# Two and four column tiles for the last attention product of pairs 4 to 31, with reciprocals spread by DMA

## The chip, the cores and the metric

The kernel runs on one core of a Trainium2 chip. The metric is the device time of one execution in microseconds (us); the median of three timed runs stands for a kernel. Engine names as in the profile: PE is TensorE (PEld its weight loads), DVE VectorE, ACT ScalarE, POOL GpSimd, SP SyncE, whose queue (SPq) issues all transfers of this kernel but two.

## What is computed

Linear attention with 8 batches, 8 heads, 576 tokens and head size 64, then a feed-forward layer over all 4608 tokens, all in float32:

```python
q_p, k_p = phi(q), phi(k)        # 128 features: exp(x @ omega.T - |x|^2/2 - row maximum)
kv  = einsum('bhsm,bhsd->bhmd', k_p, v)
z   = sum(k_p, axis=2)
num = einsum('bhsm,bhmd->bhsd', q_p, kv)
den = einsum('bhsm,bhm->bhs', q_p, z)[..., None] + 1e-06
x   = (num / den)                # heads side by side: 4608 x 512
h   = x @ w_in                   # 512 -> 2048
out = (h * erf(softplus(h))) @ w_out
```

## The kernel before

**Work.** Attention goes by pairs of heads: 32 pairs, numbered n = 4 * batch + p. The feed-forward layer goes by six blocks of tokens (`SUPERS`; the first two have 576 tokens each, the others 864), each in four quarters of the hidden size; it is most of TensorE's work. Its matmuls are float32r in three terms (high x high, high x low, low x high), with tiles h, hX, hY, hZ for the first product and o, oX, oY, oZ for the second. The attention's matmuls are float32.

**One pair.** `load` brings q, k and v; `project` makes the features (tiles ppk, ppq in PSUM; after the exponential fk, fq in SBUF). `key_values` multiplies the features of the keys with v and a column of ones into the PSUM tile kvp: for each head 64 columns of values and one column, z. It does so in two column tiles, the array's left half for features 0 to 63, its right half for 64 to 127. `kvhigh` copies kvp into the SBUF tile kh, with z repeated 64 times for each head, so that kh is 2 x 128 columns. `turn` transposes fq in three steps (pt in PSUM, qh in SBUF, 128 features x 1152 tokens of the two heads).

**The last product, which the change touches**, is in `attend`. There are four products for each pair, one for each head j and half t of its tokens (`SPANS`: 288 each): weights kh[:, j] (128 features x 128 columns), moving qh (288 columns). The result nd, a PSUM bank, holds 64 rows of numerators and 64 equal rows of denominators. `log_den` takes the logarithm of the 64 denominator rows and writes it to the other 64 partitions, those of the numerators, in the SBUF tile rc; `exp_den` takes exp(-x) of both heads' at once; `divide` multiplies the numerators in PSUM by it into xs, on 64 partitions at a time.

```python
def log_den(self, rc, nd, j, w):
    num, den = rows(j)
    act.activation(rc.ap[num], nd.ap[den, :w], AF.Ln, bias=eps[den])
def divide(self, x, nd, rc, j, o, c, w):
    num = rows(j)[0]
    dve.tensor_mul(x.ap[num, o:o + w], nd.ap[num, c:c + w], rc.ap[num, c:c + w])
```

`split` makes high and low parts (xh, xl, xc) of xs for a block of tokens, before the first product of that block.

**What sets the order.** Every step is declared with `pl.op`: the engines that may do it and the time that it is thought to take, what it reads and writes, and for some a due time (`plan`). `Plan.order` runs a list schedule over all steps when the program is built: each engine takes the ready step that is due first, steps without a due time get theirs from their successors, and a step that needs a buffer waits for a free one (`SLOTS`, `CAPS`; kh and qh have one buffer each). Each engine then carries out its steps in the order found, in order. SyncE's queue is ordered in the same way; weight fetches may be issued up to `AHEAD` = 40.09 us before they are due, and the time of a transfer is taken from `BANDWIDTH`. `JITTER` adds a fixed pseudo-random perturbation to the due times in the stretches that it lists.

The due time of an attention step is `pair_time(n, x)`: the start of pair n's period plus x times the period (at most 33 us) times 1.2. The period is 33.4 us for pairs 4 to 7, 20.7 for 8 to 15, 42.1 for 16 to 19, 24.5 for 20 to 27 and 40.9 for 28 to 31; pairs 0 to 3, before the feed-forward layer begins, have 11.4. The four products of pair n are due at x = 0.75, 0.80, 0.85 and 0.90, key_values at 0.28, turn from 0.5 on. PSUM has 8 banks.

Of the kernel before, what the change touches and what calls it, by code (L numbers as in the profile page):

```python
# [71 lines left out]


COST = dict(mm=0.132, proj=0.222, half=0.156, tr=0.109, kv=1.35, table=1.3)
BANDWIDTH = 270e3
LAG = {"T": 0.33914999999999995, "A": 0.258, "V": 0.24975, "G": 0.2994, "S": 0.3024}
SLOTS = dict(w=8, g=11, u=2, f=2, mx=3, sq=3, v=1, qh=1, ql=1, kh=1, kl=1, xs=12, xh=2, xl=2,
             os=4, ps=8)
# [239 lines left out]
def whole_(n):  # L318
# [1 line left out]
    return n < WHOLE or WHOLE2[0] <= n < WHOLE2[1]  # L320


JITTER = ((186.1, 206.1, 4, 581), (227.5, 727.5, 4, 5), (648.5, 748.5, 1, 6), (712.0, 762.0, 2, 7),
# [34 lines left out]
AHEAD = 40.09  # L358

SPANS = ((0, 288), (288, 288))  # L360
# [16 lines left out]
BY = 30.39  # L377
RPOOL = SPOOL = "g"
VOS = 5
TAIL = [("V", 0.69, -1e9)]  # L380
LATE = 52.68
LOADS = 1e9
# [9 lines left out]
def build(emit):  # L392
# [246 lines left out]
    def key_values(n, t0):  # L639
        a = pairs[n]  # L640
        f, v = a["fk"], a["v"]
        kvp = a["kvp"] = pl.tile("ps", "kvp" + a["nm"], [P, 512], F32, "att", early(n))
        pl.op("kv", [("T", COST["kv"], -1e9)], lambda e: E.key_values(kvp, f, v),
              reads=[(f, i) for i in range(NC)] + [(v, 0)], writes=[(kvp, 0)], plan=pair_time(n, t0))
        whole = whole_(n)
        kh = a["kh"] = pl.tile("kh", "kh" + a["nm"], [P, 2, P], F32 if whole else F32R)
        kl = a["kl"] = kh if whole else pl.tile("kl", "kl" + a["nm"], [P, 2, P], F32R)
        pl.op("kvhigh", [("V", 0.6, -1e9), ("A", 0.7, -1e9)], lambda e: E.kv_high(e, kh, kvp),
              reads=[(kvp, 0)], writes=[(kh, 0)])
        if not whole:  # L650
            pl.op("kvrest", [("V", 0.6, -1e9)], lambda e: E.kv_rest(kl, kvp, kh),
                  reads=[(kvp, 0), (kh, 0)], writes=[(kl, 0)])

    def turn(n, t0):
# [5 lines left out]
        for i in range(3):  # L660
# [5 lines left out]
            if not whole:  # L666
                pl.op("turnrest", [("V", 0.56, -1e9)], lambda e, i=i, pt=pt: E.turn_rest(ql, qh, pt, i),
                      reads=[(pt, 0), (qh, i)], writes=[(ql, i)])

    def attend(n, t0):  # L670
        a = pairs[n]
        for t, (c0, w) in enumerate(SPANS):
            rc = pl.tile(f"rc{t}", f"rc{a['nm']}_{t}", [P, w])
            nds = [pl.tile("ps", f"nd{a['nm']}_{j}_{t}", [P, 512], F32, "att", early(n)) for j in range(2)]
            for j, nd in enumerate(nds):
                c = range((j * S + c0) // 384, (j * S + c0 + w - 1) // 384 + 1)
                pl.op("nd", [("T", w / 600 if whole_(n) else 3 * max(0.111, 0.012 + w / 2400), -1e9)],
                      lambda e, j=j, c0=c0, w=w, nd=nd:
                      E.attend(nd, a["kh"], a["kl"], a["qh"], a["ql"], j, c0, w),
                      reads=[(a["kh"], 0), (a["kl"], 0)] + [(a["qh"], i) for i in c]  # L680
                      + [(a["ql"], i) for i in c], writes=[(nd, 0)],
                      plan=pair_time(n, t0 + 0.1 * t + 0.05 * j))
            for j, nd in enumerate(nds):
                pl.op("ndlog", [("A", 0.25 + 0.00083 * w, -1e9)],
                      lambda e, j=j, w=w, nd=nd, rc=rc: E.log_den(rc, nd, j, w),
                      reads=[(nd, 0)], writes=[(rc, j)], set="exp")
            pl.op("ndexp", [("A", 0.2 + 0.00083 * w, -1e9)], lambda e, rc=rc: E.exp_den(rc),
                  reads=[(rc, 0), (rc, 1)], writes=[(rc, 0), (rc, 1)], set="exp")
            for i, h, o, at0, n0 in pieces(a["b"], c0, w):
                k = (i, a["p"], h)  # L690
                if k not in xs:
                    xs[k] = pl.tile("xs", "xs%d_%d_%d" % k, [P, SUPERS[i][0]]), []
                x, keys = xs[k]
                for j, nd in enumerate(nds):
                    key = (n, t, at0, j)
                    keys.append(key)
                    pl.op("divide", [("V", 0.15 + 0.00105 * n0, -1e9)],
                          lambda e, j=j, x=x, o=o, at0=at0, n0=n0, nd=nd, rc=rc:
                          E.divide(x, nd, rc, j, o, at0, n0),
                          reads=[(nd, 0), (rc, j)], writes=[(x, key)],  # L700
                          plan=pair_time(n, t0 + 0.1 * t) + DIVIDE)
# [35 lines left out]
    def attention(n):  # L737
        if n == 0:
            load(0, "k")
            project(0, "k", 0.0)  # L740
            load(0, "q")
        project(n, "q", 0.15)
        if n + 1 < N:
            load(n + 1, "k")
        key_values(n, 0.28)
        if n + 1 < N:
            project(n + 1, "k", 0.0)
            load(n + 1, "q")
        turn(n, 0.5)
        attend(n, 0.75)  # L750


    gran = {}
# [276 lines left out]
def tile_attention_moe(ctx: ExitStack, tc: tile.TileContext, qT, kT, qR, kR, qN, kN, vP, omT, w1, w2, out):  # L1030
# [68 lines left out]
    class Emit:  # L1099
# [140 lines left out]
        def kv_rest(self, kl, kvp, kh):  # L1240
            for (dst, src), (hi, _) in zip(self.kv_parts(kvp, kl), self.kv_parts(kvp, kh)):
                dve.tensor_sub(dst, src, hi.bitcast(F32))

        def turn(self, pt, f, i):
            for c in range(3):
                pe.transpose(out=pt.ap[:, c * P:(c + 1) * P], in_=f.ap[:, 3 * i + c, :], identity=ident)
# [162 lines left out]
```

## Time and profile before

| | before |
|---|---|
| runs, us | 1014.33, 1015.59, 1019.1 |
| median, us | 1015.59 |
| span of the profiled execution, us | 1013.4 |
| PE, DVE, ACT, POOL busy | 98%, 78%, 69%, 63% |
| bytes moved by DMA | 235.87 MB |
| mean granted TensorE clock | 0.998 |

The profile shows one execution. Its span runs from its first instruction to its last; its time as the runs count it isn't given beside it, so the span is set against the median. Busy time of an engine is the time covered by its instructions; for PE the ends of matmuls are modelled and overlap, so steps from start to start say more than durations. A float32 matmul appears as two records, a float32r matmul and a transpose as one.

### The profile page before, as it was taken

The numbers are of one execution on the slowest core, as the hardware profiler recorded it, in microseconds if no ns is written. First come the engines' busy times: TensorE is split into PE (matmuls) and PEld (weight loads), VectorE is DVE, ScalarE is ACT, GpSimd is POOL, SyncE is SP. The second block draws the span as 40 slices with busy tenths as digits, with TensorE's granted clock in tenths as the row PEclk, the third lists the DMA queues.
The fourth block names the chain that finished last, engine by engine and source line by source line (L and its number), as shares of the span: only waits on it lengthen the run. The fifth ranks groups of instructions, "written<-read, shape, count | busy, mean of one in ns | idle before, by whom it ended". The sixth has DMA issues, their size and how long they took to land.

```text
span 1013.4 us, 19460 instructions
## 1 busy us (share of the span) xinstructions
PE 995.4 (98%) x7108; PEld 926.1 (91%) x7108; DVE 788.7 (78%) x1278; ACT 695.3 (69%) x1307; POOL 636.1 (63%) x477
## 2 busy tenths in 40 slices
PE   8999999999999999999999999999999999999998
PEld 7899889989999899999999899999999999999997
DVE  5799878996677878676897778789787788687654
ACT  7979787686785975766768685868548665746560
POOL 3535433866668857475894848489575687677530
PEclk9999999999999999999999999999999999999999
DMA  8376778588687597576766867676677556686761
GB/s 214 102 254 245 254 237 325 192 306 302 227 279 240 166 320 289 186 279 230 256 215 216 310 228 226 217 226 204 225 274 242 186 177 219 227 293 213 232 205 70
DMA packets 102366, 235.87 MB, mean 233 GB/s; under 512 B 11520, under 2 KB 12032, under 8 KB 102272
## 3 DMA queue, kind: packets, MB, share of 16 engines
q1 hardware_dynamic: 102112, 234.57, 69.2%
q8 instruction: 57, 0.93, 0.4%
q14 instruction: 37, 0.30, 0.1%
q10 hardware_dynamic: 160, 0.07, 0.0%
HBM read 191.59 MB, written 42.99 MB: 231 GB/s over the span
## 4 chain that ended last, share of the span: by engine, by line
PE 88%; DVE 6%; DMA 4%; ACT 1%; SPq 1%; issue 1%; DVEq 0%; ACTq 0%
PE hX L1047 15%; PE o L1047 14%; PE oX L1047 12%; PE h L1047 8%; PE hY L1047 7%; PE oY L1047 6%; PE nd L1047 5%; PE ppq L1047 4%; PE hZ L1047 4%; PE ppk L1047 3%; PE kvp L1047 3%; PE oZ L1047 3%; PE pt L1047 2%; DMA st<-w 2%; DVE st L1047 1%; DMA uk<-kT 1%
## 5 line engine op out<-in xcount | busy, mean ns | idle before, releaser
L1047 PE MATMUL o<-gh,w 128*128 128x288 f32 (+1 forms) x704 | 176.0, 324 | 3.3 <-DVE w L1047 1.8
L1047 PE MATMUL hX<-xh,wb 128*128 128x432 f32 x512 | 171.4, 368 | 0.0
L1047 POOL TENSOR_TENSOR hs<-gs,hs 128x864 f32<-128x864 f32 (+1 forms) x44 | 95.5, 2190 | 94.5 <-ACT gs L1047 83.0
L1047 PEld LDWEIGHTS o<-gh,w 128*128 128x128 f32 x704 | 122.4, 189 | 8.2 <-DVE w L1047 2.5
L1047 PE MATMUL h<-xh,w 128*128 128x288 f32 x512 | 123.4, 312 | 2.2 <-ACT w L1047 1.0
L1047 PE MATMUL o<-gl,w 128*128 128x288 f32 (+1 forms) x352 | 110.3, 313 | 0.0
L1047 PE MATMUL oX<-th,wb 128*128 128x432 f32 x312 | 101.4, 364 | 0.0
L1047 PEld LDWEIGHTS hX<-xh,wb 128*128 128x128 f32 x512 | 96.2, 188 | 5.2 <-DVE hs L1047 0.2
L1047 PE MATMUL hX<-xl,wb 128*128 128x432 f32 x256 | 91.8, 359 | 0.7 <-DVE xl L1047 0.7
L1047 PEld LDWEIGHTS h<-xh,w 128*128 128x128 f32 x512 | 86.8, 189 | 5.9 <-ACT w L1047 1.2
L1047 POOL TENSOR_TENSOR uq<-uq 128x288 f32<-128x288 f32 (+1 forms) x50 | 45.7, 934 | 72.8 <-DMA uq<-qN 31.8
L1047 ACT ACT_TABLE_LOAD x68 | 87.2, 1283 | 1.9 <-PEq L1400 0.7
L1047 PE MATMUL hY<-xh,wb 128*128 128x432 f32 x256 | 88.2, 372 | 0.0
L1047 ACT ACTIVATE fk<-ppk,mxk 128x128 f32<-128x128 f32 x288 | 81.9, 378 | 5.7 <-DVE mxk L1047 5.2
L1047 ACT ACTIVATE fq<-ppq,mxq 128x128 f32<-128x128 f32 x288 | 78.2, 384 | 8.0 <-DVE mxq L1047 7.5
L1047 ACT ACTIVATE rc<-nd,eps 64x288 f32<-64x288 f32 x128 | 63.5, 496 | 27.7 <-PE nd L1047 25.1
L1047 PE MATMUL nd<-qh,kh 128*128 128x288 f32 x256 | 78.0, 409 | 3.8 <-DVE qh L1047 2.9
L1047 DVE TENSOR_TENSOR xs<-nd,rc 64x288 f32<-64x288 f32 (+1 forms) x160 | 61.6, 393 | 24.6 <-ACT rc L1047 17.8
L1047 ACT ACTIVATE hs<-hX 128x432 f32<-128x432 f32 x64 | 33.8, 531 | 67.4 <-PE hX L1047 63.3
L1047 POOL TENSOR_TENSOR tl<-gs,th 128x864 fp32r<-128x864 f32 x32 | 71.1, 2241 | 9.7 <-ACT th L1047 3.5
L1047 PE MATMUL h<-xl,w 128*128 128x288 f32 x256 | 75.7, 296 | 0.0
L1047 ACT ACTIVATE gs<-hs 128x1728 f32<-128x1728 f32 (+1 forms) x48 | 69.0, 1479 | 0.3
(144 smaller groups left out, 2770.3 us busy)
## 6 DMA issues: line engine op xcount, KB each, us to landing
wb<-wdc SPq DMA_DIRECT2D x232, 256.0 KB, 3.8
wb<-wdw SPq DMA_DIRECT2D x174, 256.0 KB, 3.9
w<-wdw SPq DMA_DIRECT2D x44, 512.0 KB, 6.2
st<-w SPq DMA_DIRECT2D x32, 512.0 KB, 6.0
wdw<-w SPq DMA_DIRECT2D x32, 512.0 KB, 5.0
wdc<-c SPq DMA_DIRECT2D x32, 512.0 KB, 4.6
v<-vP SPq DMA_DIRECT2D x32, 325.0 KB, 4.6
uk<-kR SPq DMA_DIRECT2D x24, 320.0 KB, 4.7
```

What stands on the lines that cost most here:

```text
L1047: return tc.keep_in_program_order(method(*args, **kwargs))
```

## The change

- For pairs 4 to 31 (`n >= APART`) the last product is taken apart. kh is now 128 numerator columns (64 for each head) and 64 columns that hold z of each head 32 times.
- `denominators`: four matmuls of 32 columns, one for each head and half of the tokens, in four column tiles, into one PSUM bank dn. One logarithm and one exponential follow over all 128 partitions x 288. The result is stored in DRAM (147,456 bytes) and read back by two transfers, one for each head, each of which puts the two rows of that head on 64 partitions (tile rb).
- `numerators`: for each half of the tokens two matmuls of 64 columns, one for each head, in two column tiles, into one bank; then one multiplication (or more, where a block of tokens ends within) on all 128 partitions. They are due at x = 1.15 and 1.25 and are declared after the key_values of the next pair. Their banks count apart from the others' (at most two).
- `BANDWIDTH` goes from 270e3 to 310e3, and the list in `JITTER` is another: 31 entries in place of 115. So the order of all steps changes.

```diff
-BANDWIDTH = 270e3
+BANDWIDTH = 310e3
...
+APART = 4
+NDCAP = 2
+NUM0 = 1.15
...
+        if n >= APART:
+            kh = a["kh"] = pl.tile("kh", "kh" + a["nm"], [P, 3 * D])
+            pl.op("kvhigh", [("V", 0.49, -1e9), ("A", 0.45, -1e9)], lambda e: E.kv_apart(e, kh, kvp),
+                  reads=[(kvp, 0)], writes=[(kh, 0)])
+            return
...
+    def denominators(n, t0):
...
+        pl.op("nd", [("T", 0.49, -1e9)], lambda e: E.denominators(dn, a["kh"], a["qh"], w),
+              reads=everything, writes=[(dn, 0)], plan=pair_time(n, t0))
+        rc = pl.tile("rc0", "rc" + a["nm"], [P, w])
+        pl.op("ndlog", [("A", 0.5, -1e9)], lambda e: E.log_dens(rc, dn, w), reads=[(dn, 0)],
+              writes=[(rc, 0)], set="exp")
+        pl.op("ndexp", [("A", 0.44, -1e9)], lambda e: E.exp_den(rc), reads=[(rc, 0)], writes=[(rc, 0)],
+              set="exp")
+        rd = pl.tile("wdr" + a["nm"], "wdr" + a["nm"], [P, w])
+        pl.op("rstore", [("S", 0.1, 1e9)], lambda e: E.fetch(rd.ap, rc.ap), reads=[(rc, 0)],
+              writes=[(rd, 0)], size=P * w * 4)
+        rb = pl.tile("rb", "rb" + a["nm"], [P, 2, w])
+        for j in range(2):
+            pl.op("rfetch", [("S", 0.1, 1e9)], lambda e, j=j: E.spread(rb, rd, j), reads=[(rd, 0)],
+                  writes=[(rb, j)], size=P * w * 4)
+        a["rb"] = rb
+
+    def numerators(n, t0):
...
+        for t, (c0, _) in enumerate(SPANS):
+            nd = pl.tile("ps", f"nd{t}{a['nm']}", [P, 512], F32, "nd" if NDCAP else "att", NDCAP or early(n))
+            pl.op("nd", [("T", 0.49, -1e9)],
+                  lambda e, c0=c0, nd=nd: E.numerators(nd, a["kh"], a["qh"], c0, w),
+                  reads=everything, writes=[(nd, 0)], plan=pair_time(n, t0 + 0.1 * t))
...
     def attend(n, t0):
+        if n >= APART:
+            denominators(n, t0)
+            return
...
         key_values(n, 0.28)
+        if n > APART:
+            numerators(n - 1, NUM0)
...
         attend(n, 0.75)
+        if n + 1 == N:
+            numerators(n, NUM0)
...
+        def denominators(self, dn, kh, qh, w):
+            r = D // 2
+            for g in range(4):
+                c = P + g // 2 * r
+                pe.matmul(dn.ap[g * r:(g + 1) * r, :w], lhsT=kh.ap[:, c:c + r],
+                          rhs=qh.ap[:, g * w:(g + 1) * w], start=True, stop=True)
+
+        def numerators(self, nd, kh, qh, c0, w):
+            for j in range(2):
+                c = slice(j * S + c0, j * S + c0 + w)
+                pe.matmul(nd.ap[j * D:(j + 1) * D, :w], lhsT=kh.ap[:, j * D:(j + 1) * D],
+                          rhs=qh.ap[:, c], start=True, stop=True)
+
+        def log_dens(self, rc, dn, w):
+            act.activation(rc.ap, dn.ap[:, :w], AF.Ln, bias=eps)
+
+        def spread(self, rb, rd, j):
+            rows = rd.ap.rearrange("(j t r) c -> j r t c", j=2, t=2)[j, 0:1]
+            sp.dma_start(rb.ap[j * D:(j + 1) * D], rows.broadcast_to([D, 2, rows.shape[-1]]))
+
+        def divide_both(self, x, nd, rb, t, o, c, w):
+            dve.tensor_mul(x.ap[:, o:o + w], nd.ap[:, c:c + w], rb.ap[:, t, c:c + w])
```

## Rows read from the trace of the kernel before

**Rows 1.** The page's first part: span, then busy time of each engine.

```profile
span 1013.4 us, 19460 instructions
PE 995.4 (98%) x7108; PEld 926.1 (91%) x7108; DVE 788.7 (78%) x1278; ACT 695.3 (69%) x1307; POOL 636.1 (63%) x477
```

**Rows 2.** Busy time by stretches: length, each engine, granted clock, DMA share, GB/s.

```profile
50.00:200.00 150.00, 144.79 (x1238) 137.73 (x1239) 130.12 (x223) 116.83 (x246) 74.20 (x68) 0.99 0.72 250
200.00:355.00 155.00, 152.40 (x1351) 141.97 (x1350) 121.46 (x227) 114.59 (x254) 110.62 (x103) 1.00 0.74 253
355.00:835.00 480.00, 480.00 (x3244) 440.86 (x3241) 382.34 (x615) 333.55 (x606) 330.56 (x226) 1.00 0.71 237
```

**Rows 3.** TensorE in order of time around three last products: start, duration, instructions.

```profile
516.88 0.36 PE L1047 MATMUL hY<-xl,wb 128*128 128x432 f32 x1
517.08 0.35 PE L1047 MATMUL hY<-xh,wb 128*128 128x432 f32 x1
517.27 0.65 PE L1047 MATMUL nd<-qh,kh 128*128 128x288 f32 x2
517.54 0.57 PE L1047 MATMUL hY<-xh,wb 128*128 128x432 f32 x1
517.95 0.36 PE L1047 MATMUL hY<-xl,wb 128*128 128x432 f32 x1
...
522.17 0.36 PE L1047 MATMUL hY<-xh,wb 128*128 128x432 f32 x1
522.37 1.14 PE L1047 MATMUL nd<-qh,kh 128*128 128x288 f32 x4
523.12 0.57 PE L1047 MATMUL hY<-xh,wb 128*128 128x432 f32 x1
523.54 0.36 PE L1047 MATMUL hY<-xl,wb 128*128 128x432 f32 x1
```

**Rows 4.** The same view around one kvp; its last two records apart.

```profile
503.08 0.35 PE L1047 MATMUL oY<-bh,wb 128*128 128x432 f32 x1
503.36 1.38 PE L1047 MATMUL kvp<-v,fk 128*64 128x130 f32 x36
504.51 0.23 PE L1047 MATMUL kvp<-v,fk 128*64 128x65 f32 x2
504.67 0.46 PE L1047 MATMUL oZ<-bh,wb 128*128 128x432 f32 x1
504.97 0.35 PE L1047 MATMUL oZ<-bl,wb 128*128 128x432 f32 x1
```

**Rows 5.** The same view: first and last run of nd, pairs 4 to 31.

```profile
60.30 0.65 PE L1047 MATMUL nd<-qh,kh 128*128 128x288 f32 x2
...
831.08 0.65 PE L1047 MATMUL nd<-qh,kh 128*128 128x288 f32 x2
```

**Rows 6.** Groups of ScalarE: form, count, busy us, mean ns, idle before.

```profile
L1047 ACT ACTIVATE rc<-nd,eps 64x288 f32<-64x288 f32 x128 | 63.5, 496 | 27.7 <-PE nd L1047 25.1
L1047 ACT ACTIVATE rc<-rc 128x288 f32<-128x288 f32 x64 | 28.4, 444 | 2.0
```

**Rows 7.** Groups of VectorE, the multiplications.

```profile
L1047 DVE TENSOR_TENSOR xs<-nd,rc 64x288 f32<-64x288 f32 x96 | 43.4, 453 | 19.7 <-ACT rc L1047 15.8 <-PE nd L1047 1.9
L1047 DVE TENSOR_TENSOR xs<-nd,rc 64x144 f32<-64x144 f32 x64 | 18.3, 302 | 4.9 <-ACT rc L1047 2.0 <-PE nd L1047 1.9
```

**Rows 8.** DMA: packets, the main queue, two kinds of issue (median us to landing).

```profile
DMA packets 102366, 235.87 MB, mean 233 GB/s; under 512 B 11520, under 2 KB 12032, under 8 KB 102272
q1 hardware_dynamic: 102112, 234.57, 69.2%
wdw<-w SPq DMA_DIRECT2D x32, 512.0 KB, 5.0
uq<-qT SPq DMA_DIRECT2D x3, 96.0 KB, 2.8
```

**Rows 9.** TensorE's waits from 50 to 355 us, first and last of eleven.

```profile
PE o L1047 <- DVE w L1047: 1.8, 3, 1.0
...
PE hZ L1047 <- ACT fq L1047: 0.2, 1, 0.2
```

**Rows 10.** In order of time, VectorE and TensorE near 352 us.

```profile
349.64 2.98 DVE L1047 TENSOR_TENSOR xl<-xc,xh 128x1728 fp32r<-128x1728 f32 x1
...
351.66 0.35 PE L1047 MATMUL hX<-xh,wb 128*128 128x432 f32 x1
352.68 0.46 PE L1047 MATMUL hX<-xl,wb 128*128 128x432 f32 x1 [0.67 <-DVE xl L1047]
```

**Rows 11.** VectorE's waits: us in total, times, longest.

```profile
DVE xs L1047 <- ACT rc L1047: 17.8, 19, 2.2
```

More of the change, by code (lines that the diff above doesn't have):

```diff
@@ L320, in whole_ @@
     return n < WHOLE or WHOLE2[0] <= n < WHOLE2[1]
-JITTER = ((186.1, 206.1, 4, 581), (227.5, 727.5, 4, 5), (648.5, 748.5, 1, 6), (712.0, 762.0, 2, 7),
[34 rows of a table removed]
+JITTER = ((126.7, 226.7, 8, 485), (605.4, 615.4, 4, 265), (421.4, 471.4, 8, 168),
[10 rows of a table added]
 AHEAD = 40.09
@@ L668, in turn, with place, bank @@
                       reads=[(pt, 0), (qh, i)], writes=[(ql, i)])
+    def place(n, t, c0, w, nds, part):
+        a = pairs[n]
+        for i, h, o, at0, n0 in pieces(a["b"], c0, w):
+            k = (i, a["p"], h)
+            if k not in xs:
+                xs[k] = pl.tile("xs", "xs%d_%d_%d" % k, [P, SUPERS[i][0]]), []
+            part(k, i, o, at0, n0)
+    def denominators(n, t0):
+        a = pairs[n]
+        w = SPANS[0][1]
+        everything = [(a["kh"], 0)] + [(a["qh"], i) for i in range(3)]
+        def bank(name):
+            return pl.tile("ps", name + a["nm"], [P, 512], F32, "att", early(n))
+        dn = bank("dn")
+        pl.op("nd", [("T", 0.49, -1e9)], lambda e: E.denominators(dn, a["kh"], a["qh"], w),
[13 more added lines that the diff above has]
+        a["rb"] = rb
@@ new lines, in numerators, with part @@
+    def numerators(n, t0):
+        a = pairs[n]
+        w, rb = SPANS[0][1], a["rb"]
+        everything = [(a["kh"], 0)] + [(a["qh"], i) for i in range(3)]
+        for t, (c0, _) in enumerate(SPANS):
[3 more added lines that the diff above has]
+                  reads=everything, writes=[(nd, 0)], plan=pair_time(n, t0 + 0.1 * t))
+            def part(k, i, o, at0, n0, t=t, nd=nd):
+                x, keys = xs[k]
+                keys.append((n, t, at0))
+                pl.op("divide", [("V", 0.15 + 0.00105 * n0, -1e9)],
+                      lambda e: E.divide_both(x, nd, rb, t, o, at0, n0),
+                      reads=[(nd, 0), (rb, 0), (rb, 1)], writes=[(x, keys[-1])],
+                      plan=pair_time(n, t0 + 0.1 * t) + DIVIDE)
+            place(n, t, c0, w, nd, part)
@@ L1242, in kv_rest, with kv_apart @@
                 dve.tensor_sub(dst, src, hi.bitcast(F32))
+        def kv_apart(self, e, kh, kvp):
+            s = kvp.ap[:, :2 * P].rearrange("p (j d) -> p j d", j=2)[:, :, :D1]
+            copy(e, kh.ap[:, :P].rearrange("p (j d) -> p j d", j=2), s[:, :, :D])
+            copy(e, kh.ap[:, P:].rearrange("p (j d) -> p j d", j=2),
+                 s[:, :, D:].broadcast_to([P, 2, D // 2]))
+        def denominators(self, dn, kh, qh, w):
[16 more added lines that the diff above has]
+            dve.tensor_mul(x.ap[:, o:o + w], nd.ap[:, c:c + w], rb.ap[:, t, c:c + w])
         def turn(self, pt, f, i):
```

44 rows, old and new, of the table JITTER are left out of this document.

## The prediction

> **What bounds the kernel now.** I read the page's first part, then busy time by stretches, then the order of time around two places. The page and the stretches [rows 1, 2]: TensorE is busy 995.4 of 1013.4 us, and from 355 to 835 us it is busy 480.00 of 480.00 at the full granted clock. In the two stretches before, from 50 to 355 us, it stands still for 5.2 + 2.6 = 7.8 us in all. VectorE and ScalarE have a quarter of their time free. So whatever adds a microsecond to TensorE's own sequence adds one to the end, and whatever frees another engine can give back 7.8 us at most outside the first 50 us, which pairs 0 to 3 fill and the change leaves alone.
>
> Next, the price of one last product [rows 3]. The float32r matmuls around it step by 0.20 us. From hY at 517.08 to the second hY after it at 517.95 lie 0.87 us, which hold two such steps and one product: 0.47. From 522.17 to 523.54 lie 1.37 us with two products: 0.97, so 0.485 each. That is 288 float32 columns at 1.68 ns, and nothing is lost on the way in or out. The records last 0.40 us each and overlap; only starts are used.
>
> Then the one place where the kernel already uses two column tiles, kvp [rows 4]. From oY at 503.08 to the second oZ at 504.97 lie 1.89 us; without two steps, 1.49. Each half of the array takes one product of 130 columns and eight of 65, 650 columns, 1.09 us at 1.68 ns; the halves in turn would need 2.19. So they run together, and 0.40 us is lost around them. Part of the loss is seen at the ends. kvp starts 0.28 after oY, 0.08 more than a step. Its last records start at 504.51 and need some 0.055 for half a product of 65 columns, but oZ starts at 504.67: 0.105. The next oZ comes after 0.30, 0.10 more than a step. Together 0.285. The rest, 0.115, is first-weight time or a small loss in each of nine steps. A full-width product between full-width neighbours pays none of this. I take 0.34 us for one visit to a tiled arrangement of long products, between 0.285 and 0.40.
>
> The Trainium skill ("TensorEngine Tiling (Array Packing)", Tiling Modes) says that changing the tiling mode, not just the tile, drains TensorE, and in its Overview that columns of at most 32 allow up to four times the speed. By that speed alone the sum below would be 13.6 us less time; the trace agrees with the drain as well, at 0.285 to 0.40 us a visit, which turns the sign.
>
> **TensorE's columns.** A pair now has four products, 1.94 us [rows 3]. Afterwards it has three steps of 288 columns: the four denominators side by side, and twice two numerators side by side. If tiles run fully together that is 1.455 us. Over 28 pairs: 54.3 before, 40.7 after, -13.6 us. Two halves at full speed are shown by kvp, though both halves read the same columns there; four, each with other columns, are not shown. If they ran two and two, the denominators cost 0.97 and 13.6 us come on top; one after the other, 40.7 on top. Nothing excludes either, but the nearest row runs together, so I take 0.485.
>
> **TensorE's visits.** The three steps of a pair are due at 0.75, 1.15 and 1.25 of its period, so they stand apart unless the order happens to join them: 84 visits at most. How often neighbours join can be counted now: the 112 products of pairs 4 to 31 stand in 86 runs, the first at 60.30 and the last at 831.08 [rows 5], so 26 of 84 neighbours, 31%, are joined, with dues 0.05 of a period apart. The two numerator steps are due 0.1 apart; I take 13%, 4 joins. By the file's due times, in the 20 pairs whose period is under 34 us, numerators(n-1) is due about 1 us after key_values(n), which is in the same two-column arrangement; 31% of those is 6 joins. That leaves 74 visits x 0.34 = 25.2 us. Bounds: 28 visits x 0.285 = 8 and 84 x 0.40 = 34. Net TensorE: 25.2 - 13.6 = +11.6 us, between -6 and +20.
>
> **ScalarE and VectorE.** Now a pair has four logarithms of 496 ns and two exponentials of 444 [rows 6]; afterwards one of each at full height, for which I take the same times: 1.93 us less, 54 us over 28 pairs. Multiplications take 43.4 + 18.3 us, 1.93 us a pair [rows 7]; at full height there are half as many, 27 us less in all. The copy of kvp loses half of its second part. None of this is on the path from 355 us on. Of the 7.8 us before that I give back 3.
>
> **DMA.** Each of the 28 pairs stores 147 KB and reads it back twice: 84 transfers, 12.4 MB, 5.3% of the 235.87 MB that the page counts; the queue's share of 69.2% [rows 8] becomes some 73%. SyncE's queue is in order, so the store waits there for the exponential and the two reads for the store, with weight fetches queued behind. Those are issued up to 40 us ahead, and from 50 to 355 us TensorE's eleven kinds of wait, 8.0 us in all, end with VectorE or ScalarE and none with a transfer [rows 9]. I cost this at nothing; the cover is that lead, and without it TensorE would pay the store's landing, 2.8 to 5.0 us [rows 8], for each pair.
>
> **Added waits and moved steps.** The numerators leave pair n for a place after key_values(n+1). TensorE does not wait there for the reciprocals, since its matmuls read kh and qh alone; the multiplication on VectorE does. From the denominators on that is 0.50 + 0.44 on ScalarE and two landings, from 2.8 (96 KB) to 5.0 us (512 KB): 6.5 to 10.9 us, against a distance in due time of 0.4 of a period x 1.2: 9.9 us in pairs 8 to 15, 11.8 in 20 to 27, 15.8 in the others. It fits, with little to spare; behind a late multiplication stand all of VectorE's drains of PSUM. kh and qh have one buffer, so kvhigh(n+1) and the first turn copy now wait for numerators(n); TensorE passes those in order, and kh is needed 0.47 of a period later. xs is complete 10 to 16 us later. That bites at the change of token blocks: at 351.66 hX already waits 0.67 us for an xl that VectorE ends at 352.6 [rows 10]. For five such changes I add 2 us in all, from 0 to 8.
>
> **Order.** The bandwidth constant and the perturbations change the whole order. What it can take away are the 7.8 us above; what it adds could be as much. I take nothing, 8 us either way.
>
> **Sum.** -13.6 + 25.2 - 3 + 2 = +10.6 us. The profiled span of 1013.4 becomes 1024.0; the median of the runs, 1015.6, is 2.2 above that span, so 1026 us.
>
> **Rivals.**
> (a) The order joins the steps. With 40 visits in all, 1.4 a pair, the change breaks even on TensorE. The least is 28: the four-column step needs a visit of its own, and both numerator steps are entered from kvp; 28 x 0.34 = 9.5, a gain of 4. With the 3 us given back these are 1012.6 and 1008.5, and the order's 8 us around them. Below 34 visits it is faster by 0.5%. For it: 31% of neighbours join today. Against: the dues of the two numerator steps are twice as far apart as those of today's neighbours.
> (b) The gain on the other engines about cancels the visits: all 7.8 us come back and a visit costs 0.285 (74 x 0.285 = 21 us): 21 - 13.6 - 7.8 = 0, 1015. Against: nothing outside 50 to 355 us can come back.
> (c) The reciprocals come late. If queueing on ScalarE and SyncE adds 3 us in the 16 pairs with 9.9 to 11.8 us, VectorE stands still for up to 48 us, and with half of it passed on through PSUM TensorE loses 24: 1050; with a quarter, 1038. For it: the multiplications already wait 17.8 us for ScalarE's reciprocals now [rows 11]. Against: that is 0.9 us at a time, and the dues leave 9.9 us.
> (d) Four streams of different columns don't run together: 13.6 us more, 1040. Against it kvp, for two.
>
> **How the numbers follow.** My forecast 0.46 (1019 to 1034), (a) 0.17, (b) 0.14, (c) 0.15, (d) 0.08. The time is 1026. The range takes the forecast, (b), (d), nearly all of (a) and the lower part of (c): 1007 to 1042. A difference under 0.5% (5 us) can't be told from no change here. Faster by more than that: two thirds of (a), 0.11, and with the order's 8 us some of (b), 0.06: 0.17. Within 0.5%: the rest of (a), 0.06, of (b), 0.08, and the forecast's low end, 0.05: 0.19. Slower: 0.64.
>
> **What would show it.** In the profile after: nd's and the denominators' starts 0.485 us apart for full 288 columns with neighbours 0.3 us late around them, some 74 separate tiled visits besides kvp's; TensorE still near 98% busy; ScalarE some 54 and VectorE some 27 us less; no TensorE wait for DMA. I am wrong if the steps stand side by side (fewer than 40 visits), if a visit costs under 0.2 us with 288 columns, or if TensorE shows new waits on VectorE's drains.

## The result and the profile after

| | before | after |
|---|---|---|
| runs, us | 1014.33 to 1019.1 (4) | 1022.99, 1026.25, 1026.36, 1027.67 |
| median, us | 1016.37 | 1026.3 |
| ratio, 95% interval | | 1.0095 [1.0067, 1.0123] |
| profiled span, us | 1013.4 | 1021.2 |

The change costs 10 us, 1.0%. A fourth run of the kernel before, 1017.14, is counted in here. The profiled execution of after is the one of 1022.99, the lowest of the four; the spans of the others are 1024.5 to 1025.9. Of all runs below one, 1046.53 us of e10 at a mean granted clock of 0.907, is in the slower state and left out of its median.

The page's first part of after, beside [rows 1]:

```profile
span 1021.2 us, 19871 instructions
PE 1002.1 (98%) x7332; PEld 899.5 (88%) x7332; DVE 776.3 (76%) x1226; ACT 649.4 (64%) x1200; POOL 637.5 (62%) x457
```

ScalarE and VectorE have 46 and 12 us less to do; TensorE is at 98% as before, over a longer span. Busy time by stretches, beside [rows 2]:

```profile
50.00:200.00 150.00, 144.38 (x1270) 132.20 (x1269) 123.25 (x220) 111.25 (x230) 71.94 (x63) 0.99 0.80 268
200.00:355.00 155.00, 153.87 (x1404) 137.36 (x1402) 113.15 (x206) 104.30 (x232) 105.52 (x94) 0.99 0.79 271
355.00:835.00 480.00, 479.42 (x3348) 419.96 (x3347) 373.46 (x575) 304.34 (x536) 326.41 (x220) 1.00 0.76 248
```

From 355 to 835 us TensorE is as full as before (479.42 of 480), with ScalarE 29 and VectorE 9 us lighter: freed time on engines that weren't the bound. TensorE in order of time around one step of numerators and one of denominators, beside [rows 3]:

```profile
575.46 0.36 PE L1092 MATMUL hY<-xl,wb 128*128 128x432 f32 x1
575.66 0.35 PE L1092 MATMUL hY<-xh,wb 128*128 128x432 f32 x1
575.94 0.71 PE L1092 MATMUL nd<-qh,kh 128*64 128x288 f32 x4
576.58 0.46 PE L1092 MATMUL hZ<-xh,wb 128*128 128x432 f32 x1
576.88 0.35 PE L1092 MATMUL hZ<-xl,wb 128*128 128x432 f32 x1
...
641.82 0.36 PE L1092 MATMUL oX<-th,wb 128*128 128x432 f32 x1
642.11 0.69 PE L1092 MATMUL dn<-qh,kh 128*32 128x288 f32 x8
642.73 0.46 PE L1092 MATMUL oX<-th,wb 128*128 128x432 f32 x1
643.03 0.35 PE L1092 MATMUL oX<-tl,wb 128*128 128x432 f32 x1
```

Numerators: from 575.66 to 576.88 lie 1.22 us; two float32r steps of 0.20 and one step of 288 float32 columns, 0.485, are 0.88, so 0.34 is lost. Denominators: 641.82 to 643.03 are 1.21, again 0.33 lost, although eight records, four products of different columns, lie in that one step. So four column tiles do run together, and each visit pays on the way in (the start comes 0.08 to 0.09 later than a step) and on the way out.

**A ledger of TensorE.** I took every step from start to start, subtracted the time of its columns, and counted what is over around a run of tiled products as the visit's loss (the median of its kind), all else as the rest: waits, and columns at half clock (the last section shows such a stretch; each of 3.4 us costs some 1.7). The rest is what is left over, so the ledger always adds up.

| profiled execution | columns | visits: loss (count) | rest | first to last matmul |
|---|---|---|---|---|
| before | 947.2 | 34.6 (80) | 23.6 | 1005.4 |
| after | 933.8 | 55.3 (127) | 24.0 | 1013.0 |

The 7.6 us between the two are -13.4 of columns, +20.7 of visits and +0.4 of the rest (rounded).

### The profile page after: what moved, and what is told of

Its sections match the earlier page's. It is cut to its first block, busy times and chain, and to the rows that moved or that the text cites. A ratio compares the mean times of both kernels' runs of the same rounds, so it can differ in the third digit from the quotient of the medians.

```text
span 1021.2 us, 19871 instructions
## 1 busy us (share of the span) xinstructions
PE 1002.1 (98%) x7332; PEld 899.5 (88%) x7332; DVE 776.3 (76%) x1226; ACT 649.4 (64%) x1200; POOL 637.5 (62%) x457
## 3 DMA queue, kind: packets, MB, share of 16 engines
q1 hardware_dynamic: 114208, 246.96, 73.5%
## 4 chain that ended last, share of the span: by engine, by line
PE 89%; DVE 7%; DMA 2%; issue 1%; ACT 1%; SPq 0%; DVEq 0%
PE o L1092 15%; PE hX L1092 14%; PE oX L1092 12%; PE h L1092 10%; PE hY L1092 7%; PE oY L1092 6%; PE ppq L1092 5%; PE ppk L1092 4%; PE nd L1092 4%; PE kvp L1092 4%; PE hZ L1092 3%; PE oZ L1092 3%; PE pt L1092 2%; PE dn L1092 2%; DVE gs L1092 1%; DVE hs L1092 1%
## 5 line engine op out<-in xcount | busy, mean ns | idle before, releaser
L1092 PE MATMUL o<-gh,w 128*128 128x288 f32 (+1 forms) x704 | 169.1, 319 | 2.2 <-ACT w L1092 1.2
L1092 PE MATMUL hX<-xh,wb 128*128 128x432 f32 x512 | 166.5, 366 | 0.7 <-DVE hs L1092 0.7
L1092 POOL TENSOR_TENSOR hs<-gs,hs 128x864 f32<-128x864 f32 (+1 forms) x50 | 102.9, 2080 | 101.7 <-ACT gs L1092 78.8
L1092 PE MATMUL h<-xh,w 128*128 128x288 f32 x512 | 119.0, 308 | 3.4 <-DVE w L1092 1.9
L1092 POOL TENSOR_TENSOR uq<-uq 128x288 f32<-128x288 f32 (+1 forms) x46 | 41.6, 924 | 80.0 <-DMA uq<-qN 40.0
L1092 POOL TENSOR_TENSOR tl<-gs,th 128x864 fp32r<-128x864 f32 x34 | 80.1, 2378 | 18.3 <-ACT th L1092 9.0
L1092 PE MATMUL hY<-xh,wb 128*128 128x432 f32 x256 | 83.8, 365 | 0.0
L1092 ACT ACTIVATE gs<-gs 128x1728 f32<-128x1728 f32 (+1 forms) x48 | 69.0, 1481 | 0.3
L1092 PEld LDWEIGHTS o<-gl,w 128*128 128x128 f32 x352 | 66.8, 190 | 0.8
L1092 DVE TENSOR_TENSOR os<-oX,os 128x432 f32<-128x432 f32 x86 | 51.0, 602 | 20.2 <-PE oX L1092 20.1
```

Source lines behind the costliest of these rows:

```text
L1092: return tc.keep_in_program_order(method(*args, **kwargs))
```

## The experiments

The times are medians; the ratios are to the kernel before on the same chip (1016.58 for e1, e3, e4 and e5, 1014.96 for e2, e6 and e7, 1015.93 for e8 to e10). The ledger of all of them:

| run | median | ratio [95%] | profiled span | visits (count) | rest |
|---|---|---|---|---|---|
| e1 before, new order | 1037.38 | 1.0197 [1.0144, 1.025] | 1035.5 | 35.7 (78) | 44.6 |
| e2 after, old order | 1054.47 | 1.0376 [1.0346, 1.0406] | 1055.7 | 56.4 (127) | 56.9 |
| e3 before, split columns | 1041.9 | 1.0254 [1.0238, 1.027] | 1038.9 | 67.5 (165) | 16.3 |
| e4 after, full width | 1011.11 | 0.9947 [0.9928, 0.9965] | 1006.9 | 34.7 (80) | 29.5 |
| e5 after, no transfers | 1022.03 | 1.0063 [1.0044, 1.0082] | 1019.6 | 55.3 (127) | 22.5 |
| e6 numerators beside kvp | 1020.81 | 1.0051 [1.0028, 1.0075] | 1018.5 | 43.7 (104) | 32.8 |
| e7 also denominators beside ppq | 1026.5 | 1.0115 [1.0075, 1.0154] | 1023.0 | 39.1 (81) | 41.8 |
| e8 as e6, order made for it | 1017.77 | 1.0023 [1.0005, 1.004] | 1011.1 | 43.0 (100) | 26.0 |
| e9 as e8, another order | 1022.72 | 1.0074 [1.0053, 1.0096] | 1021.2 | 42.0 (95) | 37.1 |
| e10 as e7, order made for it | 1025.92 | 1.0088 [1.0059, 1.0118] | 1024.6 | 38.8 (79) | 43.8 |

Columns are 947.2 us in e1 and e3, 933.8 in all others.

**e3: what does a visit cost, with nothing else changed?** Before's kernel in before's order; each last product becomes two half-width ones side by side over the same columns.

```diff
-                pe.matmul(nd.ap[:, :w], lhsT=kh.ap[:, j, :], rhs=qh.ap[:, c], start=True, stop=True)
+                for h in (slice(0, D), slice(D, P)):
+                    pe.matmul(nd.ap[h, :w], lhsT=kh.ap[:, j, h], rhs=qh.ap[:, c], start=True, stop=True)
```

> The kernel before with each of its last products issued as two products of 64 weight columns side by side, over the same 288 columns, in the same order: the column time stays, and 90 visits to the two-column arrangement come in. Theory: a visit costs 0.345 us as in the trace after, four of them in the first 50 us: 28 to 31 us more, 1044 to 1047 us. Rival (a visit is hidden, or its cost belongs to kvp's short products): within 5 us of the kernel before.

25.3 us slower. TensorE around one product of e3:

```profile
530.33 0.35 PE L1047 MATMUL hY<-xh,wb 128*128 128x432 f32 x1
530.61 0.71 PE L1047 MATMUL nd<-qh,kh 128*64 128x288 f32 x4
531.25 0.46 PE L1047 MATMUL hY<-xh,wb 128*128 128x432 f32 x1
531.55 0.36 PE L1047 MATMUL hY<-xl,wb 128*128 128x432 f32 x1
```

530.33 to 531.55 is 1.22 us where [rows 3] have 0.87. The median over the 62 single products that stand alone is 0.354 lost. In all, visits cost 33 us more, so the price is real. 7 us of the rest went away: 1.7 of them is the one stretch at half clock that before has and e3 has not, 1.2 are waits (12.9 us in place of 14.1), and about 2 are waits of the first 50 us that the ledger counts as visits here. The time is 2 us below the theory's 1044 to 1047 and far from the rival's.

**e4: after without the visits.** The same steps in the same order, same columns, full width.

```diff
...
-            r = D // 2
-            for g in range(4):
-                c = P + g // 2 * r
-                pe.matmul(dn.ap[g * r:(g + 1) * r, :w], lhsT=kh.ap[:, c:c + r],
-                          rhs=qh.ap[:, g * w:(g + 1) * w], start=True, stop=True)
+            pe.matmul(dn.ap[:, :w], lhsT=kh.ap[:, P:2 * P], rhs=qh.ap[:, :w], start=True, stop=True)
...
-            for j in range(2):
-                c = slice(j * S + c0, j * S + c0 + w)
-                pe.matmul(nd.ap[j * D:(j + 1) * D, :w], lhsT=kh.ap[:, j * D:(j + 1) * D],
-                          rhs=qh.ap[:, c], start=True, stop=True)
+            pe.matmul(nd.ap[:, :w], lhsT=kh.ap[:, :P], rhs=qh.ap[:, c0:c0 + w], start=True, stop=True)
```

> The kernel after in the same order, but each of its three steps is one full-width product over 288 columns: same column time, no visits, and the transfers and the work of the other engines stay. It leaves out the numerators of each pair's second head and three of the four denominators. Theory: the 20.8 us that the visits of these steps cost in the trace after go, 1003 to 1008 us, faster than the kernel before by about 1%. Rival (the order, the transfers or late reciprocals make it slower): 1022 us or more.

15.2 us faster than after, and 5.4 faster than before. TensorE around one numerator product of e4:

```profile
541.70 0.35 PE L1092 MATMUL oX<-th,wb 128*128 128x432 f32 x1
541.89 0.65 PE L1092 MATMUL nd<-qh,kh 128*128 128x288 f32 x2
542.16 0.58 PE L1092 MATMUL oZ<-bh,wb 128*128 128x432 f32 x1
542.58 0.36 PE L1092 MATMUL oZ<-bl,wb 128*128 128x432 f32 x1
```

541.70 to 542.58 is 0.88 us, two steps and the columns, where after has 1.22. The 20.6 us of visits are gone (34.7, as in the kernel before), and the rest is 5.5 us more, mostly waits (18.8 us in place of 14.6): three quarters of what TensorE is given reach the end. It falls between the two expectations, near the theory's. Since e4 leaves out part of the result, it is no version to use.

**e5: after without the transfers.** A constant takes the place of rb.

```diff
-        pl.op("rstore", [("S", 0.1, 1e9)], lambda e: E.fetch(rd.ap, rc.ap), reads=[(rc, 0)],
+        pl.op("rstore", [("S", 0.1, 1e9)], lambda e: None, reads=[(rc, 0)],
...
-            dve.tensor_mul(x.ap[:, o:o + w], nd.ap[:, c:c + w], rb.ap[:, t, c:c + w])
+            dve.tensor_mul(x.ap[:, o:o + w], nd.ap[:, c:c + w], ones[:, c:c + w])
```

> The kernel after in the same order without the three transfers for each pair; the multiplication takes a constant in place of the reciprocals, so that it waits for none. It leaves out the division. Theory: the transfers and the wait for the reciprocals are hidden, 1024 to 1028 us. Rival (late reciprocals hold VectorE, or the transfers hold SyncE's queue): 1020 us or less.

4.3 us faster than after by the medians, 1.6 by the profiled spans; visits are the same, the rest is 1.5 us less. That lies between the two expectations. The waits of TensorE are no shorter (15.3 us in place of 14.6), but e5 has one stretch at half clock where after has two, which is 1.7 us; the other runs go the same way, with a mean granted clock of 0.997 to 0.998 in e5 and 0.994 to 0.996 in after. So the transfers are not the main cost: 2 to 4 us go with them, and as far as the traces show they go with the clock and not with waits for a transfer.

**e1 and e2: the order alone.** `BANDWIDTH` and `JITTER` are exchanged: e1 is before's steps with after's two constants, e2 after's steps with before's. Of e1's edit, without the two lists (before's has 121 entries, not 115 as said above, after's 31):

```diff
-BANDWIDTH = 270e3
+BANDWIDTH = 310e3
...
```

> The kernel before with the bandwidth constant and the perturbations of the kernel after, so another order of the same work. Theory (visits to the column tiles cost more than the columns save): the order carries little, 1016 us, at most 8 us either way. Rival (the new order is what makes it slower): 1024 us or more.

> The kernel after with the bandwidth constant and the perturbations of the kernel before. The counterpart, the kernel before with the new constants, took 20 us more than the kernel before. Theory (columns -13.6 us, visits some +20 us whatever the order, and an order whose constants were not made for these steps adds waits): the visits cost 17 to 25 us again, and new waits of TensorE come on top: 1028 to 1045 us. Rival (the new constants are worse as such, for either set of steps): 1010 to 1018 us.

Both are slower than the kernel whose steps they have, by 21 and 28 us, with 1 us more of visits and 21 and 33 us more of the rest. e2's 1054.47 lies above its theory's 1028 to 1045 too. The stretch from 355 to 835 us, of e1 and of e2:

```profile
355.00:835.00 480.00, 466.00 (x3184) 424.27 (x3183) 384.45 (x595) 322.23 (x591) 297.87 (x216) 0.99 0.68 227
```

```profile
355.00:835.00 480.00, 468.30 (x3234) 407.37 (x3232) 363.44 (x564) 298.96 (x533) 313.89 (x203) 0.99 0.74 243
```

TensorE stands still for 14 and 12 us where [rows 2] have none. Each of the two orders fits the steps that it was made for and not the other's. So e1's theory of the order's share (1016, 8 us either way) was wrong, and e1's rival reads the number rightly but not its meaning: the new order isn't worse in itself, it is worse for other steps. These two runs can't tell how good the orders are for their own steps; the ledger can (23.6 and 24.0 of rest).

**e6 and e7: fewer visits.** e6 puts both numerator steps of a pair into the step of the next pair's key_values, in the same two column tiles. e7 also puts the denominators ahead of the next pair's project of q, whose products are in row tiles.

```diff
...
+        def both(e):
+            E.key_values(kvp, f, v)
+            nd_products(n - 1, banks)
+        pl.op("kv", [("T", COST["kv"] + 0.49 * len(banks), -1e9)], both, reads=reads, writes=writes,
+              plan=pair_time(n, t0))
...
+            def both(e):
+                if dn is not None:
+                    E.denominators(dn, pairs[n - 1]["kh"], pairs[n - 1]["qh"], SPANS[0][1])
+                E.project_rows(banks[0], banks[2], u, qk)
```

> The kernel after with both numerator steps of pair n-1 right behind key_values of pair n, in one step of the schedule, so that they need no visit of their own (in the trace after, kvp with numerators beside it loses 0.43 us like kvp alone). The constants stay; the order shifts. Theory: all visits together lose 34.5 + 28 x 0.34 = 44 us in place of 55: 1015 us, 6 us either way for the order. Rival (numerators cost more than their columns wherever they stand, or the kernel is held by something else): 1022 us or more.

> The kernel before this one (numerators beside kvp), and the denominators of pair n-1 right ahead of the projection of pair n's queries, which is in row tiles, for 24 pairs. In the trace after, the two together lose 0.58 us, apart 0.34 + 0.44. Theory: 24 x 0.2 = 5 us less in visits than with numerators beside kvp alone, 1010 us, but the reciprocals come some 5 us later, so 8 us either way. Rival (the later reciprocals hold VectorE and through it TensorE): above 1018 us, with waits of TensorE that VectorE ends.

TensorE around one joint step of e6, and of e7:

```profile
407.36 0.38 PE L1113 MATMUL ppq<-wr,uq 128*128 128x128 f32 x2
407.68 1.38 PE L1113 MATMUL kvp<-v,fk 128*64 128x130 f32 x36
408.88 1.14 PE L1113 MATMUL nd<-qh,kh 128*64 128x288 f32 x8
409.95 0.46 PE L1113 MATMUL o<-gh,w 128*128 128x432 f32 x1
410.25 0.36 PE L1113 MATMUL o<-gl,w 128*128 128x432 f32 x1
```

```profile
404.58 0.36 PE L1126 MATMUL hX<-xh,wb 128*128 128x432 f32 x1
404.87 0.69 PE L1126 MATMUL dn<-qh,kh 128*32 128x288 f32 x8
405.50 1.16 PE L1126 MATMUL ppq<-wr,uq 64*128 64x128 f32 x16
406.59 0.46 PE L1126 MATMUL o<-gh,w 128*128 128x432 f32 x1
406.89 0.35 PE L1126 MATMUL o<-gl,w 128*128 128x432 f32 x1
```

By the medians of the ledger kvp with nd loses 0.435 us, kvp alone 0.425: the numerators ride for nearly nothing. dn with ppq loses 0.58, where dn alone (0.34) and ppq alone (0.44) lose 0.78. So e6 saves 11.6 us of visits and e7 16.2 against after, as counted. But e6 shows 8.8 us more of the rest and e7 17.8, of which about 3 us each are more columns at half clock. e6 ends 5.5 us ahead of after, at the upper edge of its theory's 1009 to 1021 and below its rival; e7 ends level with after. In e7 the saving went whole into the rest, at the time that its rival gave: TensorE's waits are 26.1 us in place of 14.6, and those that VectorE ends 14.7 in place of 7.3. VectorE's multiplication waits for rb 17.4 us in place of 7.4, but none of TensorE's waits ends with the multiplication, so that the late reciprocals are the reason isn't shown.

**e8 to e10: are those waits a matter of order?** e6's kernel with the measured times entered and a list of perturbations made for it (e8), another such list (e9), and e7's kernel with one of its own (e10).

```diff
...
-COST = dict(mm=0.132, proj=0.222, half=0.156, tr=0.109, kv=1.35, table=1.3)
+COST = dict(mm=0.132, proj=0.222, half=0.161, tr=0.109, kv=1.49, table=1.3)
...
-        pl.op("nd", [("T", 0.49, -1e9)], lambda e: E.denominators(dn, a["kh"], a["qh"], w),
+        pl.op("nd", [("T", 0.83, -1e9)], lambda e: E.denominators(dn, a["kh"], a["qh"], w),
...
```

> The kernel of e6 (both numerator steps of a pair right behind the key_values of the next), with the times that the traces showed entered in the list schedule (key_values 1.49 us, a step of project's two half-height products 0.161, the denominators with their visit 0.83) and a list of perturbations of the due times made for these steps. Theory: the visits stay at the 46 us that e6 showed, and what e6 lost was the 31 us of other waits, which an order made for these steps brings back to the some 20 us of the kernels before and after. Then 1020.8 - 11 = 1010, between 1005 and 1014, faster than before by 0.2% to 1%. Rival: the waits are those of the steps themselves (the numerators wait for banks and for the late reciprocals), no order removes them, and the time stays at 1018 to 1024.

> As e8, with another list of perturbations, which by the list schedule's own times ends 3 us later. Theory: the schedule's own times tell orders apart only roughly; two orders made for the same steps stand within 6 us of each other on the chip, in either direction, and both below e6's 1020.8. Rival: as for e8, 1018 to 1024.

> The kernel of e7 (numerators behind the next pair's key_values, denominators ahead of its project of q), with the same times entered and a list of perturbations made for it. Theory: visits of 40 us as in e7, 6 us less than in e8, and waits of some 20 to 25 us in place of 40: 1007 to 1014, at most 3 us from e8. Rival: the step that holds denominators and project of q together waits for the turn of one pair and the load of the next, so waits stay at 35 to 40 us and the time is 1020 to 1027.

Neither side has it whole. e8's profiled execution has 26.0 us of rest in place of e6's 32.8 (the ledger's figure, where the expectation says 31) and a span of 1011.1, 2.3 below before's. Of these 6.8 us, 5.1 are stretches at half clock: e6 has four of 3.4 us each, e8 one; TensorE's waits fell only from 18.5 to 16.4. Its median, 1017.77, misses the theory's 1005 to 1014: the 12 runs reach from 1013.24 to 1023.63, and the profiled one is the lowest. e9, the same steps, has 37.1 us of rest and e10 43.8, as much as e7: there the rivals' times came true. e9 is within 6 us of e8, as expected, but not below e6. Two orders made for the same steps thus stand 5 us apart, and making one doesn't reliably remove the waits; that the steps themselves cause them, as the rivals say, isn't shown. Why e8's runs scatter by 10 us, where before's 17 runs beside them reach from 1012.73 to 1019.71, stays open. e8 is 8.5 us faster than the change and still 0.2% slower than before: no version that computes the whole result beats before.

## Why the prediction came out, step by step

**Columns, -13.6 predicted, -13.4 by the ledger.** Four streams of different columns run together, which no row of before showed; rival (d) is out.

**Visits, 25.2 predicted, 20.7 measured.** The price was right, 0.34 each: denominators alone lose 0.341 (15 times), one numerator step alone 0.354 (23), two together 0.356 (4). What was off is how many stand alone. The 84 steps form 75 separate runs, since nine pairs of numerator steps joined and not four. Five of the runs stand beside kvp, where the prediction had six, so by its way of counting there are 70 visits and not 74, which is 1.4 us. Only 42 of the 70 stand by themselves. I counted a join only between products of the same arrangement; but 18 runs stand beside ppk or ppq, in 12 visits that lose 0.58 to 0.74 in place of 0.44 and another 0.34 for each run, and in five places dn stands beside nd, where both together lose 0.50. The Trainium skill ("TensorEngine Tiling (Array Packing)", Tiling Modes) says that a change of the mode drains TensorE and a change of the tile alone does not. By that the joint kvp and nd should lose one visit's time, and they do (0.43); the second change in dn, then nd costs 0.16 us here, half of what leaving for full width and coming back costs.

**ScalarE and VectorE, 54 and 27 us less, off the path.** Groups of ScalarE and VectorE in after, beside [rows 6, 7]; two of each are the new form, the 64-partition ones belong to pairs 0 to 3:

```profile
L1092 ACT ACTIVATE rc<-dn,eps 128x288 f32<-128x288 f32 x28 | 14.5, 517 | 9.5 <-PE dn L1092 6.5 <-ACT fk L1092 2.9
L1092 ACT ACTIVATE rc<-rc 128x288 f32<-128x288 f32 x36 | 16.0, 446 | 1.1
L1092 ACT ACTIVATE rc<-nd,eps 64x288 f32<-64x288 f32 x16 | 7.9, 496 | 0.6 <-PE nd L1092 0.2
```

```profile
L1092 DVE TENSOR_TENSOR xs<-nd,rb 128x288 f32<-128x288 f32 x40 | 17.4, 450 | 6.0 <-DMA rb<-wdr 5.4 <-PE nd L1092 0.6
L1092 DVE TENSOR_TENSOR xs<-nd,rb 128x144 f32<-128x144 f32 x32 | 8.3, 298 | 2.4 <-DMA rb<-wdr 2.0 <-PE nd L1092 0.4
L1092 DVE TENSOR_TENSOR xs<-nd,rc 64x288 f32<-64x288 f32 x16 | 7.2, 452 | 0.4
```

Reciprocals: 91.9 to 38.4 us, 53.5 less. Multiplications: 61.7 to 32.9, 28.8 less. Both as predicted. The engines' sums fell by less, 46 and 12 us, so the new order put other work on them. What I expected back from this, 3 us from 50 to 355 us, isn't to be seen: TensorE stood still there for 7.8 us, and stands 6.8 now. So rival (b), for which all 7.8 come back, is out.

**DMA, nothing predicted, 2 to 4 us by e5.** Transfers of after, the multiplication's wait and SyncE's:

```profile
q1 hardware_dynamic: 114208, 246.96, 73.5%
```

```profile
rb<-wdr SPq DMA_DIRECT2D x56, 144.0 KB, 5.7
wdr<-rc SPq DMA_DIRECT2D x28, 144.0 KB, 3.0
```

```profile
DVE xs L1092 <- DMA rb<-wdr: 7.4, 14, 1.5
SPq L1092 <- ACT rc L1092: 46.7, 19, 5.2
```

The share (73.5%) and the landings (3.0 and 5.7 us for 2.8 to 5.0) are near the estimate, and no wait of TensorE ends with a transfer. SyncE's queue stands 46.7 us for ScalarE's exponentials, up to 5.2 at a time; that is off TensorE's path. The multiplication waits for rb 14 times, 0.5 us each, not in every pair: rival (c), late reciprocals, is there with 7.4 of the up to 48 us that it gave VectorE. Of e5's 4.3 us the profiled executions show 1.6, the stretch at half clock that e5 doesn't have; the other runs have no trace, only their clock.

**Later xs, 2 us predicted, none seen.** No wait of TensorE in after ends with xh, xl or xc; the one in [rows 10] is gone. What is there is a wait of another kind. VectorE and TensorE in order of time in after:

```profile
196.06 1.19 DVE L1092 TENSOR_SCALAR st<-st 128x512 int32<-128x512 int32 x1 [0.74 <-DMA st<-w]
197.17 1.42 DVE L1092 TENSOR_REDUCE ppk<-ppk 128x4 f32<-128x512 f32 x2
198.76 0.89 DVE L1092 TENSOR_TENSOR xs<-nd,rb 128x288 f32<-128x288 f32 x3 [0.17 <-DMA rb<-wdr]
```

```profile
197.25 0.55 PE L1092 MATMUL pt<-ident,fq 128*128 128x128 f32 x3 [0.58 <-ACT qh L1092]
199.27 0.40 PE L1092 MATMUL h<-xh,w 128*128 128x288 f32 x1 [1.47 <-DVE xs L1092]
```

The first product h stands in the middle of its block, whose last xl was done by 178 us, so it doesn't wait for its inputs; I read the wait as one for the PSUM bank that the multiplication gives back. That multiplication was late mostly by VectorE's queue: a reduction ran until 198.6, and rb held it up for 0.17 us only. In e5, without rb, the same wait is 0.42 us, and no half clock follows it. With 0.5 us before a pt these are 2.0 us of waits for the multiplication. New waits on VectorE's drains were named as a sign of being wrong; they are there, but small, and TensorE's waits that VectorE ends are 7.3 us in both kernels.

**Order, nothing, 8 us either way.** For the change as made it came to nothing (rest +0.4). As a bound it was far too narrow: e1, e2, e7 and e9 moved the rest by 13 to 33 us. The prediction had no reason for taking nothing, and that it held is partly luck; by e1 and e2 it needs that each of the two kernels ran with constants that fit its steps.

**The sum.** 1024.0 was predicted for the profiled span, 1021.2 measured: visits 4.5 less, columns 0.2 and the rest 1.4 more. The median is 5.1 above that span, where I added 2.2. So the mechanism and the sign were right, and that the median lands on 1026 is luck: two errors of 3 us that cancel. Rival (a) needed fewer than 40 visits; e6 to e8 show that it can be had (e6's visits cost 9.1 us more than before's, (a) had 9.5), and that it is worth less than its 1008.5, because the rest is 2 to 18 us larger than before's.

## What to carry to other kernels

Price a tiled product by visits first: 0.34 to 0.36 us each here against 0.485 saved per step of 288 columns, so splitting a product that was one uninterrupted step can pay only where the pieces stand beside a product that is already tiled; here even that did not come out faster than before. Count columns and visits from start to start in one ledger with a rest; it shows whether a saving reached the end or turned into waits, and the granted clock shows how much of the rest is half clock. After a change of steps a hand-fitted order can be worth tens of microseconds less (21 and 28 here); make it anew before judging the change, with several orders, since two made for the same steps stood 5 us apart.

## What the runs showed of the hardware that was not expected

**An instruction of VectorE that lasted as long as GpSimd's.** In e1 TensorE stood still for 8.38 us at 511. VectorE, GpSimd and TensorE in order of time:

```profile
506.41 12.54 DVE L1023 TENSOR_TENSOR xl<-xs,xh 128x432 fp32r<-128x432 f32 x1
518.88 0.59 DVE L1023 TENSOR_TENSOR os<-oZ,os 128x432 f32<-128x432 f32 x1
```

```profile
506.46 1.13 POOL L1023 TENSOR_TENSOR xl<-xs,xh 128x432 fp32r<-128x432 f32 x1
507.55 4.05 POOL L1023 TENSOR_TENSOR xl<-xc,xh 128x864 fp32r<-128x864 f32 x2
511.56 3.97 POOL L1023 TENSOR_TENSOR hs<-gs,hs 128x864 f32<-128x864 f32 x2
515.48 2.14 POOL L1023 TENSOR_TENSOR gs<-hs 128x432 f32<-128x432 f32 x2
```

```profile
519.53 0.73 PE L1023 MATMUL hX<-xh,wb 128*128 128x432 f32 x1 [8.38 <-DVE os L1023]
```

The subtraction of VectorE, 1.2 us on the mean in after, took 12.54, for as long as GpSimd went from one instruction to the next. In the trace of before a tensor_scalar of VectorE, 0.43 us in the median, takes 4.73 at 194.0 in the same way. The Trainium skill ("SBUF — State Buffer", SBUF: two separate sides) says that the two engines share a port pair that one instruction holds for its whole length while the other blocks. The trace agrees on the blocking, but here it lasted over several instructions of GpSimd, not one. That the port is the cause was not tried by itself. Here a drain of PSUM (os) was queued behind it, and TensorE waited for that; in before's order the longest of VectorE's xl of this form is 1.56 us.

**Half clock after a wait.** Granted clock by stretches of after (length, PE busy, clock, DMA share, GB/s), just behind the waits of 0.58 and 1.47 us above:

```profile
195.00:199.00 4.00, 2.22 (x24) 1.00 0.83 269
200.00:203.00 3.00, 3.00 (x15) 0.50 0.92 371
203.50:206.00 2.50, 2.50 (x23) 1.00 0.93 369
```

From 199.9 to 203.3 us TensorE has half its clock (1.2 of 2.4 GHz) though it is busy throughout: a float32r step of 288 columns takes 0.24 us where 0.13 is usual. A second such stretch, at 145.3, follows waits of 1.2 and 0.4 us; before has one, at 109.5, behind waits of 0.7 and 1.0. Each costs some 1.7 us on top of the waits that it follows. Not every wait has one behind it: none follows the 1.5 us at 112 in after.
